# Seven-product form for half of the gate and value row blocks in a fused attention and SwiGLU kernel

## The chip, the cores and the metric

The kernel runs on one core of one Trainium2 chip. The metric is the time of one execution in device microseconds (us), median over several executions. In what follows PE is TensorE (matmuls), PEld its weight loads, DVE is VectorE, ACT is ScalarE and POOL is GpSimd. The tiles that matmuls write lie in PSUM (eight at a time in this kernel, called banks here), all other tiles of the engines in SBUF.

## The reference

A linear attention over 8 batches of 576 tokens is followed by a SwiGLU block over the 4608 tokens. The model width is 512, the hidden width 1536.

```python
# attention, per batch and head (8 x 8, 576 tokens, head size 64)
q_s = exp(q - max(q, -1)); q_s /= sum(q_s, -1)        # over the features
k_s = exp(k - max(k, 2));  k_s /= sum(k_s, 2)         # over the tokens
kv  = einsum('bhsd,bhse->bhde', k_s, v)
x   = einsum('bhsd,bhde->bhse', q_s, kv)              # -> (4608, 512)
# SwiGLU
g   = x @ w_gate                                      # (4608, 1536)
val = x @ w_val
out = (g * sigmoid(g) * val) @ w_out                  # (4608, 512)
```

## The kernel before

The kernel keeps x transposed (`xt`, features on partitions) and computes the hidden layer by 12 row blocks ("units") of 128 hidden features. One unit of 512 tokens is eight matmuls of 512 columns, a Silu on ScalarE and a multiply on VectorE:

```python
def m_unit(c0, n, m):                      # cut: splitting of n > 512
    for w, nm in ((wg, "g_ps"), (wv, "u_ps")):
        for kk in range(KT):               # KT = 4
            nc.tensor.matmul(out=p_, lhsT=w[:, kk, ms], rhs=xt[:, kk, c:c + w_], ...)
    nc.scalar.activation(out=sg, in_=g_ps, func=AF.Silu)
    nc.vector.tensor_mul(hr[:, m, r:r + w_], sg, u_ps)
```

The out-projection of 512 tokens (`o_quad`) is already done in a seven-product form: a product of two 2 x 2 block matrices takes seven block products in place of eight, if sums of blocks of both operands are made beforehand. The sums of the weight blocks (`wt`) are made once, on GpSimd; the sums of the hidden layer (`hs`) once per chunk, on VectorE. Several products add up in one PSUM bank, and some of these partial sums are wanted for themselves, so they are copied out between two products:

```python
def w_sums(eng):                           # called with GpSimd, in the stage of 448 tokens
    eng.tensor_sub(wt[:, 0], b12, b11);      eng.tensor_sub(wt[:, 1], b22, wt[:, 0])
    eng.tensor_sub(wt[:, 2], b22, b12);      eng.tensor_sub(wt[:, 3], b21, wt[:, 1])

def h_sum(Q, i, ...):                      # i = 0..3, one 128x1536 VectorE operation each

# o_quad: order of the products (each on two banks, p = 0, 1)
prod(x_, raw_h(0,0), raw_w(0,0));  ACT copies s1
prod(w,  sum_h(0),   sum_w(0));    ACT copies s5
between(0)                         # exps and casts of a later batch
prod(x_, sum_h(1),   sum_w(1));    DVE copies s2
prod(y,  raw_h(1,0), raw_w(1,0));  DVE adds
prod(x_, sum_h(2),   sum_w(2));    DVE adds s5
between(1)
prod(w,  sum_h(3),   raw_w(1,1));  DVE adds s2
prod(x_, raw_h(1,1), sum_w(3));    DVE copies
```

The frame: a prologue with the attention of batch 0, all units of batch 0 (576 tokens), a stage of 448 tokens that fills up to token 1024, and then seven chunks of 512 tokens. In each chunk the out-projection of the chunk before comes after unit 3, behind the four h sums that follow units 0 to 3. In the 448-token stage and the first five chunks ("attention chunks") the kv and x of a later batch are also computed, after units 8 and 10:

```python
chunks = [(S, 448)] + [(c, 512) for c in range(1024, n_tok, 512)]
for ci, (c0, n) in enumerate(chunks):
    # cut: steps = {8: kv_pair(b), 10: x_pair(b)} for b < B
    for m in range(MT):                    # MT = 12
        if ci > 0 and m == 4:
            o_quad(ci, between)
        m_unit(c0, n, m)
        if ci == 0 and m == 5:
            w_sums(nc.gpsimd)
        if ci > 0 and m < 4:
            h_sum(ci, m)
        if m in steps:
            steps[m]()
```

The softmax here doesn't subtract the row's maximum and nothing guards it: scores larger than these inputs give would overflow.

## Time and profile before

| | us |
|---|---|
| median of the runs | 309.9 |
| span of the profiled execution | 308.0 |
| PE busy | 302.4 |
| 448-token stage | 20.63 |
| an attention chunk | 31.87 |
| a chunk without attention | 29.89 |

Stage lengths are differences of start times in the timeline: the first matmul of the 448-token stage starts at 53.55 us, and the first one of each out-projection at 81.09, 112.96, 144.83, 176.70, 208.57 and 240.44, so the five chunks after the first out-projection have one length to the hundredth.

These lines of the page give the span and the busy time, and, last, the shares of the chain of waits (the chain of work that ended last):

```profile
span 308.0 us, 5679 instructions
...
PE 302.4 (98%) x2200; PEld 183.1 (59%) x2200; DVE 204.1 (66%) x395; ACT 144.1 (47%) x232; POOL 55.7 (18%) x42
...
PE 93%; DVE 4%; DMA 1%; ACT 0%; issue 0%
```

PE is busy 98% of the span. The list of PE's waits (waiting line, what released it, total us, times, longest) has two entries:

```profile
PE warm_ps L255 <- DVE zero L464: 1.1, 1, 1.1
PE kv L190 <- DVE vb L112: 0.2, 1, 0.2
```

So no steady-state wait exists.

The chunk is 31.87 us of 31.87 us PE. In the 448-token stage GpSimd makes the four `wt` sums, 3.09 us each.

### The profile page before, as it was taken

What the parts mean: (1) busy time and instruction counts of PE and PEld (TensorE: products, weight loads), DVE (VectorE), ACT (ScalarE), POOL (GpSimd) and SP (SyncE); (2) the same over time, 40 slices, a digit from 0 to 9 for tenths busy, and PEclk for the clock granted to TensorE, in tenths of its full rate; (3) what the DMA queues carried; (4) which work ended last, traced back from release to release, by engine and by line L of the source; (5) the groups of instructions that cost most, each with busy time, mean ns of one, the idle gap of its engine ahead of it and who ended that gap; (6) DMA issues with size and microseconds to landing.
All of it is one profiled execution on the core that took longest, in us unless ns stands there. A gap on an engine that the chain in (4) does not pass through costs nothing.

```text
span 308.0 us, 5679 instructions
## 1 busy us (share of the span) xinstructions
PE 302.4 (98%) x2200; PEld 183.1 (59%) x2200; DVE 204.1 (66%) x395; ACT 144.1 (47%) x232; POOL 55.7 (18%) x42
## 2 busy tenths in 40 slices
PE   8999999999999999999999999999999999999994
PEld 6777855454675458455844485448544764485443
DVE  3944459967867886788687768776877653664422
ACT  4753387824493439333944385347634213322300
POOL 1840014189420121102020302020200000000000
PEclk9999999999999999999999999999999999999999
DMA  7999999749019910894089506960540050006014
GB/s 262 263 185 207 250 393 391 221 89 393 24 31 203 385 59 0 177 321 180 0 165 294 217 2 144 285 247 2 119 97 0 0 121 19 0 2 136 3 34 103
DMA packets 39180, 46.39 MB, mean 151 GB/s; under 512 B 16368, under 2 KB 22384, under 8 KB 39152
## 3 DMA queue, kind: packets, MB, share of 16 engines
q1 hardware_dynamic: 33104, 41.17, 45.6%
q0 software_dynamic: 5808, 4.72, 9.8%
q8 instruction: 17, 0.28, 0.4%
q10 hardware_dynamic: 240, 0.13, 0.2%
q14 instruction: 11, 0.09, 0.1%
HBM read 37.75 MB, written 9.44 MB: 153 GB/s over the span
## 4 chain that ended last, share of the span: by engine, by line
PE 93%; DVE 4%; DMA 1%; ACT 0%; issue 0%
PE g_ps L304 31%; PE u_ps L304 30%; PE ox L383 12%; PE ow L383 6%; PE o_ps L331 5%; PE oy L383 3%; PE kv L190 3%; DMA q<-in_q_dram 1%; DVE rs L137 1%; PE o_ps L445 1%; PE xa L272 1%; DVE qs L146 1%; DVE xt L232 0%; DVE qt L112 0%; PE xz L272 0%; ACT eq L121 0%
## 5 line engine op out<-in xcount | busy, mean ns | idle before, releaser
L312 ACT ACTIVATE sg<-g_ps 128x512 f32<-128x512 f32 (+2 forms) x120 | 65.1, 554 | 124.3 <-PE g_ps L304 116.9
L313 DVE TENSOR_TENSOR hr<-sg,u_ps 128x512 bf16<-128x512 f32 (+2 forms) x120 | 74.2, 631 | 60.9 <-PE u_ps L304 60.4
L304 PE MATMUL g_ps<-xt,wg 128*128 128x512 bf16 (+2 forms) x480 | 111.6, 358 | 0.2
L304 PE MATMUL u_ps<-xt,wv 128*128 128x512 bf16 (+2 forms) x480 | 111.0, 358 | 0.0
L304 PEld LDWEIGHTS <-wv 128*128 128x128 f16 x480 | 46.9, 98 | 46.9 <-issue 0.3
L304 PEld LDWEIGHTS <-wg 128*128 128x128 f16 x480 | 45.9, 98 | 44.8 <-issue 2.2
L112 POOL CAST vb<-v 128x1152 bf16<-128x1152 f32 x14 | 19.6, 1398 | 103.5 <-DMA v<-in_v_dram 42.2
L383 PEld LDWEIGHTS <-hs 128*128 128x128 bf16 x336 | 32.9, 98 | 3.8
L383 PEld LDWEIGHTS <-hr 128*128 128x128 bf16 x252 | 24.7, 98 | 4.3
L137 DVE TENSOR_REDUCE rs<-eq 128x18 f32<-128x1152 bf16 x16 | 21.5, 1346 | 6.3 <-ACT eq L121 6.3
L146 POOL TENSOR_TENSOR qs<-eq,rr 128x1152 bf16<-128x1152 bf16 x7 | 14.8, 2121 | 58.2 <-DVE rr L141 49.1
L383 PE MATMUL ox<-wt,hs 128*128 128x256 f16 x168 | 20.6, 273 | 0.0
L121 ACT ACTIVATE eq<-q 128x1152 bf16<-128x1152 f32 x16 | 18.0, 1158 | 2.7 <-DMA q<-in_q_dram 2.6
L121 ACT ACTIVATE ek<-k 128x1152 bf16<-128x1152 f32 x16 | 18.0, 1152 | 2.0 <-DMA k<-in_k_dram 2.0
L331 PE MATMUL o_ps<-wo,hr 128*128 128x512 f16 x84 | 18.8, 379 | 0.0
L214 DVE TENSOR_SCALAR kn<-kv,kvr 64x64 bf16<-64x64 f32 x56 | 15.9, 283 | 1.3
L417 DVE COPY s<-ox 128x256 f32<-128x256 f32 x14 | 5.9, 425 | 12.8 <-PE ox L383 12.8
L146 DVE TENSOR_TENSOR qs<-eq,rr 128x1152 bf16<-128x1152 bf16 x9 | 13.5, 1498 | 0.4 <-DVE rr L141 0.2
L331 PEld LDWEIGHTS <-hr 128*128 128x128 bf16 x84 | 8.1, 98 | 9.5 <-issue 0.2
L255 PE MATMUL warm_ps<-zero 128*128 128x256 bf16 x80 | 11.2, 307 | 1.1 <-DVE zero L464 1.1
L190 PEld LDWEIGHTS <-ek 64*128 64x128 bf16 x288 | 8.4, 94 | 3.6 <-issue 2.5
L255 PEld LDWEIGHTS <-zero 128*128 128x128 bf16 x80 | 8.6, 110 | 3.1 <-DVE zero L464 1.1
(61 smaller groups left out, 230.8 us busy)
## 6 DMA issues: line engine op xcount, KB each, us to landing
q<-in_q_dram SPq DMA_DIRECT2D x16, 576.0 KB, 7.1
k<-in_k_dram SPq DMA_DIRECT2D x16, 576.0 KB, 8.5
v<-in_v_dram SPq DMA_DIRECT2D x16, 576.0 KB, 9.5
out_dram<-o_sb SPq DMA_DIRECT2D x70, 128.0 KB, 2.4
wo<-in_moe_w_out_dram POOLq DMA_DIRECT2D x3, 512.0 KB, 18.0
wg<-in_moe_w_gate_dram POOLq DMA_DIRECT2D x2, 512.0 KB, 11.1
wv<-in_moe_w_val_dram POOLq DMA_DIRECT2D x2, 512.0 KB, 12.8
wg<-in_moe_w_gate_dram POOLq DMA_DIRECT2D x2, 256.0 KB, 5.3
```

The source lines that it names most:

```text
L112: eng.tensor_copy(out=out, in_=in_)
L121: nc.scalar.activation(out=s["e" + what], in_=raw[what, b, G].rearrange("p h (t d) -> p t h d", d=64), func=AF.Exp,)
L137: nc.vector.reduce_sum(out=rs, in_=s["eq"].rearrange("p t h d -> p (t h) d"), axis=mybir.AxisListType.X)
L146: eng.tensor_mul(s["qs"].rearrange("p t (h d) -> p (t h) d", d=64), s["eq"].rearrange("p t h d -> p (t h) d"), s["rr"].to_broadcast([128, ...
L190: nc.tensor.matmul(out=s["kv"][g][:, 0:129], lhsT=s["ek"][r, t, :, :].rearrange("p h d -> p (h d)"), rhs=s["vb"][r, t, 0:129], start=(t == 0),
L214: nc.vector.tensor_scalar_mul(out_, src, sc)
L255: nc.tensor.matmul(out=ps[:, 0:256], lhsT=zero[:, 0:128], rhs=zero, start=True, stop=True)
L304: nc.tensor.matmul(out=p_[:, 0:w_], lhsT=w[:, kk, ms], rhs=xt[:, kk, c:c + w_], start=(kk == 0), stop=(kk == KT - 1),)
L312: nc.scalar.activation(out=sg[:, 0:w_], in_=g_ps[:, 0:w_], func=AF.Silu)
L313: nc.vector.tensor_mul(hr[:, m, r:r + w_], sg[:, 0:w_], u_ps[:, 0:w_])
L331: nc.tensor.matmul(out=o_ps, lhsT=hr[:, m, r0:r0 + 128], rhs=wo[:, m, :], start=(m == 0), stop=(m == MT - 1),)
L383: nc.tensor.matmul(out=dst[p][:, 0:HN], lhsT=lhs(kk, p), rhs=rhs(kk), start=start and kk == 0, stop=kk == HM - 1, skip_group_check=True,)
```

## The change

The intent is to take PE columns away. Six of the 12 units of each 512-token chunk are now computed as three "cycles", each of which makes the gate and the value of two row blocks by the seven-product form: 28 matmuls of 256 columns in place of 16 of 512. The form needs sums of gate and value weights (`gt`, once, VectorE, in the 448-token stage), sums of x (`xs`, once per chunk, GpSimd), and copies and adds of partial sums. Since the last product of a cycle accumulates into a bank from which a partial sum must first be read, it is put off (`pend`) to the middle of the next cycle, and the third one to `flush()` before the units that stay direct. A direct unit (`md`) runs inside each cycle to give the copies time. The out-projection moves to the start of each chunk, its product into y moves forward, and h sums 0, 1 and 3 move into it. The diff, cut to its core:

```diff
+    def g_sums(eng):                      # four lambdas, wg and wv blocks
+        ... eng.tensor_sub(gt[:, 0], b12, b11) ... gt[:, 3]
+    def x_sum(c0, i, eng=nc.vector): ...  # xs[0..3], 128x512 each
+    def cycle(c0, n, md, mid=None, slot=None):
+        prod(bx, wg[:, 0:2], xa(0, 0), True)
+        nc.scalar.copy(out=s1, in_=bx)
+        prod(by, wg[:, 2:4], xa(0, 1), True)
+        prod(bw, gt[:, 0], xs[0], True)
+        nc.scalar.copy(out=s5, in_=bw)
+        flush()                            # last product of the cycle before
+        nc.vector.tensor_add(s1, by, s1)
+        nc.scalar.activation(out=sa, in_=s1, func=AF.Silu)
+        ... mid(), slot()
+        direct(wg, g_ps)                   # unit md
+        prod(bx, gt[:, 1], xs[1])
+        nc.scalar.copy(out=s2, in_=bx)
+        nc.scalar.activation(out=sd, in_=g_ps, func=AF.Silu)
+        prod(bw, wv[:, 2:4], xs[3])
+        nc.vector.tensor_add(s2, bw, s2)
+        nc.gpsimd.tensor_mul(h_out(0), halves(sa), halves(s2))
+        direct(wv, u_ps)
+        prod(bx, gt[:, 2], xs[2])
+        nc.vector.tensor_add(s5, bx, s5)
+        nc.vector.tensor_mul(hr[:, md, rh:rh + 512], sd, u_ps)
+        def last():
+            prod(bx, gt[:, 3], xa(1, 1))
+            nc.scalar.activation(out=sb, in_=bx, func=AF.Silu)
+            nc.gpsimd.tensor_mul(h_out(1), halves(sb), halves(s5))
+        pend.append(last)
     # o_quad
+        between(0)                         # h sums 0 and 1, q exps, casts
+        prod(y, raw_h(1, 0), raw_w(1, 0))  # was after the s2 copy
         prod(w, sum_h(0), sum_w(0)); copies s5
-        between(0)
+        between(1)                         # k exps
         prod(x_, sum_h(1), sum_w(1)); copies s2
-        prod(y, raw_h(1, 0), raw_w(1, 0))
+        between(2)                         # h sum 3
         prod(x_, sum_h(2), sum_w(2))
     # stage of 448 tokens
+        w_adds = g_sums(nc.vector)
+            if m == 9: x_pair(2)           # was after unit 10
+            if m == 10: h_sum(1, 2); four x sums on GpSimd
+            if 4 <= m < 8: w_adds[m - 4]()
     # chunks
+            o_quad(ci, between)
+            cycle(c0, 0, 6, slot=norm_1 if att else None)
+            cycle(c0, 1, 7)
+            cycle(c0, 2, 8, mid=(lambda: kv_pair(b)) if att else None)
+            flush()
+            m_unit(c0, 512, 9)
+            if att: x_pair(b)
+            m_unit(c0, 512, 10)
+            ... four x sums on GpSimd, h_sum(ci + 1, 2)
+            m_unit(c0, 512, 11)
# cut: xt as a ring of 1536 tokens in fp16, kn in one operation per group
# in place of two, more buffers for sg and s, norm_mul of group 1 on GpSimd
```

More of the change, by code (lines that the diff above doesn't have):

```diff
@@ L49 @@
     HN = d_model // 2
+    XR = 1536
+    NS = 3
+    SD = 2 * NS * 128
     WARM = (64, 8, 8)
@@ L54 @@
     at = ctx.enter_context(tc.tile_pool(name="at", bufs=2))
-    ff = ctx.enter_context(tc.tile_pool(name="ff", bufs=3))
+    ff = ctx.enter_context(tc.tile_pool(name="ff", bufs=4))
     ob = ctx.enter_context(tc.tile_pool(name="ob", bufs=5))
-    sn = ctx.enter_context(tc.tile_pool(name="sn", bufs=1))
+    sn = ctx.enter_context(tc.tile_pool(name="sn", bufs=2))
     psp = ctx.enter_context(tc.tile_pool(name="psp", bufs=8, space=bass.MemoryType.PSUM))
@@ L67 @@
     hs = const.tile([128, 4, HM, 256], BF16, name="hs", tag="hs")
-    xt = const.tile([128, KT, n_tok], BF16, name="xt", tag="xt")
+    xt = const.tile([128, KT, XR], FP16, name="xt", tag="xt")
+    gt = const.tile([128, 4, 2, SD], FP16, name="gt", tag="gt")
+    xs = [const.tile([128, 2, 256], FP16, name=f"xs{i}", tag=f"xs{i}") for i in range(4)]
     hr = const.tile([128, MT, RING], BF16, name="hr", tag="hr")
@@ L76, in load @@
     def load(b, G, what, src, after=None):
-        raw[what, b, G] = ld.tile([128, 2, T * 64], FP32, tag=what, name=what)
+        raw[what, b, G] = ld.tile(
+            [128, 2, T * 64], FP32, tag=what, name=what, bufs=2 if what == "v" else 3
+        )
         ap = bass.AP(
@@ L206, in kn, with ring_parts, put_x @@
         if "kn" not in s:
-            s["kn"] = at.tile([128, 2, 64], BF16, tag="kn", name="kn")
-        for h in range(2):
-            r = slice(64 * h, 64 * h + 64)
-            out_, src, sc = s["kn"][r, g, :], s["kv"][g][r, r], s["kvr"][r, g:g + 1]
-            if eng is nc.scalar:
-                nc.scalar.mul(out_, src, sc)
-            else:
-                nc.vector.tensor_scalar_mul(out_, src, sc)
+            s["kn"] = at.tile([128, 2, 128], BF16, tag="kn", name="kn")
+        out_, src, sc = s["kn"][:, g, :], s["kv"][g][:, 0:128], s["kvr"][:, g:g + 1]
+        if eng is nc.scalar:
+            nc.scalar.mul(out_, src, sc)
+        else:
+            nc.vector.tensor_scalar_mul(out_, src, sc)
+    def ring_parts(c0, n, ring):
+        c1 = c0 + n
+        while c0 < c1:
+            w_ = min(c1, (c0 // ring + 1) * ring) - c0
+            yield c0 % ring, w_
+            c0 += w_
+    def put_x(eng, k0, c0, src):
+        o = 0
+        for r, w_ in ring_parts(c0, src.shape[-1], XR):
+            copy(eng, xt[:, k0, r:r + w_], src[:, o:o + w_])
+            o += w_
     def x(b, G, piece, eng=nc.scalar):
@@ L225, in x @@
                     out=xp[h][64 * g:64 * g + 64, 0:n].rearrange("p (t c) -> p t c", c=64),
-                    lhsT=s["kn"][r, g, :],
+                    lhsT=s["kn"][r, g, r],
                     rhs=s["qt"][g][r, t0:t1, :],
@@ L230, in x @@
         c0 = b * S + 64 * t0
-        copy(eng, xt[:, 2 * G, c0:c0 + n], xp[0][:, 0:n])
-        nc.vector.tensor_copy(out=xt[:, 2 * G + 1, c0:c0 + n], in_=xp[1][:, 0:n])
+        put_x(eng, 2 * G, c0, xp[0][:, 0:n])
+        put_x(nc.vector, 2 * G + 1, c0, xp[1][:, 0:n])
     def x_both(b, G, eng=nc.scalar):
@@ L273, in x_pair @@
                             out=o[64 * g:64 * g + 64, :].rearrange("p (t c) -> p t c", c=64),
-                            lhsT=s["kn"][r, g, :],
+                            lhsT=s["kn"][r, g, r],
                             rhs=s["qt"][g][r, t0:t1, :],
@@ L278, in x_pair @@
             for h, eng in ((0, nc.scalar), (1, nc.vector)):
-                copy(eng, xt[:, 2 * G + h, c0:c0 + n_a], ps[G][h][:, 0:n_a])
+                put_x(eng, 2 * G + h, c0, ps[G][h][:, 0:n_a])
         for h, eng in ((0, nc.scalar), (1, nc.vector)):
-            copy(
-                eng,
-                xt[:, h:h + 2 * NG - 1:2, c0 + n_a:c0 + S],
-                z[h].rearrange("p (g c) -> p g c", g=NG),
-            )
+            o = 0
+            for r, w_ in ring_parts(c0 + n_a, n_z, XR):
+                copy(
+                    eng,
+                    xt[:, h:h + 2 * NG - 1:2, r:r + w_],
+                    z[h].rearrange("p (g c) -> p g c", g=NG)[:, :, o:o + w_],
+                )
+                o += w_
     def kv_pair(b):
@@ L304, in m_unit @@
                     nc.tensor.matmul(
-                        out=p_[:, 0:w_], lhsT=w[:, kk, ms], rhs=xt[:, kk, c:c + w_],
+                        out=p_[:, 0:w_], lhsT=w[:, kk, ms], rhs=xt[:, kk, c % XR:c % XR + w_],
                         start=(kk == 0), stop=(kk == KT - 1),
@@ L313, in m_unit, with flush @@
             nc.vector.tensor_mul(hr[:, m, r:r + w_], sg[:, 0:w_], u_ps[:, 0:w_])
+    pend = []
+    def flush():
+        while pend:
+            pend.pop()()
+    def g_sums(eng):
+        b11, b12 = wg[:, 0:2, 0:SD], wv[:, 0:2, 0:SD]
+        b21, b22 = wg[:, 2:4, 0:SD], wv[:, 2:4, 0:SD]
+        return [
+            lambda: eng.tensor_sub(gt[:, 0], b12, b11),
+            lambda: eng.tensor_sub(gt[:, 1], b22, gt[:, 0]),
+            lambda: eng.tensor_sub(gt[:, 2], b22, b12),
+            lambda: eng.tensor_sub(gt[:, 3], b21, gt[:, 1]),
+        ]
@@ new lines, in x_sum, with halves, prod, direct @@
+    def x_sum(c0, i, eng=nc.vector):
+        r = c0 % XR
+        a11, a12 = xt[:, 0:2, r:r + 256], xt[:, 2:4, r:r + 256]
+        a21, a22 = xt[:, 0:2, r + 256:r + 512], xt[:, 2:4, r + 256:r + 512]
+        if i == 0:
+            eng.tensor_add(xs[0], a21, a22)
+        elif i == 1:
+            eng.tensor_sub(xs[1], xs[0], a11)
+        elif i == 2:
+            eng.tensor_sub(xs[2], a11, a21)
+        else:
+            eng.tensor_sub(xs[3], a12, xs[1])
+    def cycle(c0, n, md, mid=None, slot=None):
+        r, rh = c0 % XR, c0 % RING
+        m0 = 2 * n
+        def halves(t):
+            return t.rearrange("p (j c) -> p j c", j=2)
+        def prod(bank, wgt, rhs, first=False):
+            for j in range(2):
+                c = slice(128 * (m0 + j), 128 * (m0 + j) + 128)
+                for kk in range(2):
+                    nc.tensor.matmul(
+                        out=bank[:, 256 * j:256 * j + 256], lhsT=wgt[:, kk, c], rhs=rhs[:, kk, :],
+                        start=first and j == 0 and kk == 0, stop=kk == 1, skip_group_check=True,
+                    )
+        def direct(w, ps):
+            for kk in range(KT):
+                nc.tensor.matmul(
+                    out=ps, lhsT=w[:, kk, 128 * md:128 * md + 128], rhs=xt[:, kk, r:r + 512],
+                    start=(kk == 0), stop=(kk == KT - 1),
+                )
+        def xa(t, c):
+            return xt[:, 2 * c:2 * c + 2, r + 256 * t:r + 256 * t + 256]
+        def h_out(t):
+            return hr[:, m0:m0 + 2, rh + 256 * t:rh + 256 * t + 256]
+        def sg_tile():
+            return ff.tile([128, 512], FP32, tag="sg", name="sg")
+        bx, by, bw = [f_tile(n_) for n_ in ("sx", "sy", "sw")]
+        s1, s2, s5 = [sn.tile([128, 512], FP32, tag=n_, name=n_) for n_ in ("s1", "s2", "s5")]
+        prod(bx, wg[:, 0:2], xa(0, 0), True)
[5 more added lines that the diff above has]
+        nc.vector.tensor_add(s1, by, s1)
+        sa = sg_tile()
+        nc.scalar.activation(out=sa, in_=s1, func=AF.Silu)
+        if mid is not None:
+            mid()
+        if slot is not None:
+            slot()
+        g_ps, u_ps = f_tile("g_ps"), f_tile("u_ps")
+        direct(wg, g_ps)
+        prod(bx, gt[:, 1], xs[1])
+        nc.scalar.copy(out=s2, in_=bx)
+        sd = sg_tile()
+        nc.scalar.activation(out=sd, in_=g_ps, func=AF.Silu)
[8 more added lines that the diff above has]
+            prod(bx, gt[:, 3], xa(1, 1))
+            sb = sg_tile()
+            nc.scalar.activation(out=sb, in_=bx, func=AF.Silu)
+            nc.gpsimd.tensor_mul(h_out(1), halves(sb), halves(s5))
+        pend.append(last)
@@ L372, in o_quad @@
         s1, s2, s5 = [
-            [sn.tile([128, HN], FP32, tag=f"{n}{p}", name=n) for p in range(2)]
-            for n in ("s1", "s2", "s5")
+            [t[:, HN * p:HN * p + HN] for p in range(2)]
+            for t in [sn.tile([128, 512], FP32, tag=n, name=n) for n in ("s1", "s2", "s5")]
         ]
@@ L408, in o_quad @@
             nc.scalar.copy(out=s1[p], in_=x_[p][:, 0:HN])
-        for p in range(2):
-            prod(w, p, sum_h(0), sum_w(0), True)
-        for p in range(2):
-            nc.scalar.copy(out=s5[p], in_=w[p][:, 0:HN])
         between(0)
-        for p in range(2):
-            prod(x_, p, sum_h(1), sum_w(1), False)
-        for p in range(2):
-            nc.vector.tensor_copy(out=s2[p], in_=x_[p][:, 0:HN])
         for p in range(2):
@@ L422, in o_quad @@
         for p in range(2):
+            prod(w, p, sum_h(0), sum_w(0), True)
+        for p in range(2):
+            nc.scalar.copy(out=s5[p], in_=w[p][:, 0:HN])
+        between(1)
+        for p in range(2):
+            prod(x_, p, sum_h(1), sum_w(1), False)
+        for p in range(2):
+            nc.vector.tensor_copy(out=s2[p], in_=x_[p][:, 0:HN])
+        between(2)
+        for p in range(2):
             prod(x_, p, sum_h(2), sum_w(2), False)
@@ L425, in o_quad @@
             add(p, 1, 1, x_, s5)
-        between(1)
+        between(3)
         for p in range(2):
@@ L549 @@
         exp(2, 1, "k")
-        chunks = [(S, 448)] + [(c, 512) for c in range(1024, n_tok, 512)]
-        for ci, (c0, n) in enumerate(chunks):
-            b = ci + 2
-            steps = {}
-            if b < B:
-                steps = {8: lambda: kv_pair(b), 10: lambda: x_pair(b)}
-            def between(i):
-                if b >= B:
+        w_adds = g_sums(nc.vector)
+        for m in range(MT):
+            if m == 4:
+                norm_sum(2, 1)
+                norm_mul(2, 1, nc.gpsimd)
+                tr_dma(2, 1)
+                load_group(3, 0)
+                load_group(3, 1)
+            m_unit(S, 1024 - S, m)
+            if m == 5:
+                w_sums(nc.gpsimd)
+            if m == 8:
+                kv_pair(2)
+            if m == 9:
+                x_pair(2)
+            if m == 10:
+                h_sum(1, 2)
+                for i in range(4):
+                    x_sum(1024, i, nc.gpsimd)
+            if 4 <= m < 8:
+                w_adds[m - 4]()
+        n_ch = n_tok // 512 - 1
+        for ci in range(1, n_ch):
+            b, c0 = ci + 2, 512 * (ci + 1)
+            att = b < B
+            def between(i):
+                if i == 0:
+                    h_sum(ci, 0)
+                    h_sum(ci, 1)
+                elif i == 2:
+                    h_sum(ci, 3)
+                if not att:
                     return
@@ L562, in between, with norm_1 @@
                         exp(b, G, "q")
+                        cast_v(b, G, nc.gpsimd)
+                elif i == 1:
                     for G in range(NG):
                         exp(b, G, "k")
-                        cast_v(b, G, nc.gpsimd)
-                else:
+                elif i == 3:
                     norm_sum(b, 0)
                     norm_mul(b, 0, nc.gpsimd)
-            for m in range(MT):
-                if ci == 0 and m == 4:
-                    norm_sum(2, 1)
-                    norm_mul(2, 1, nc.gpsimd)
-                    tr_dma(2, 1)
-                    load_group(3, 0)
-                    load_group(3, 1)
-                if ci > 0 and m == 4:
-                    o_quad(ci, between)
-                    if b < B:
-                        tr_dma(b, 0)
-                if ci > 0 and m == 5 and b < B:
-                    norm(b, 1)
-                    tr_dma(b, 1)
-                    if b + 1 < B:
-                        load_group(b + 1, 0)
-                        load_group(b + 1, 1)
-                m_unit(c0, n, m)
-                if ci == 0 and m == 5:
-                    w_sums(nc.gpsimd)
-                if ci > 0 and m < 4:
-                    h_sum(ci, m)
-                if m in steps:
-                    steps[m]()
+                    tr_dma(b, 0)
+            def norm_1():
+                norm_sum(b, 1)
+                norm_mul(b, 1, nc.gpsimd)
+                tr_dma(b, 1)
+                if b + 1 < B:
+                    load_group(b + 1, 0)
+                    load_group(b + 1, 1)
+            o_quad(ci, between)
[4 more added lines that the diff above has]
+            m_unit(c0, 512, 9)
+            if att:
+                x_pair(b)
+            m_unit(c0, 512, 10)
+            if ci + 1 < n_ch:
+                for i in range(4):
+                    x_sum(c0 + 512, i, nc.gpsimd)
+                h_sum(ci + 1, 2)
+            m_unit(c0, 512, 11)
         last = n_tok // 128 - 4
```

## The prediction

> **What bounds the kernel now.** TensorE. The page gives PE 302.4 us busy of a 308.0 us span at granted clock 1.0. PE's own waits sum to about 1.3 us, and the chain of waits is 93% PE. In the timeline a 512-column matmul follows the next every 0.216 us (0.863 per four), a 256-column one every 0.109 (1.31 per twelve): only fewer columns or new stalls move the time. A chunk with attention takes 31.87 us, one without 29.9. VectorE (66%), ScalarE (47%) and GpSimd (18%) are hidden behind eight PSUM banks.
>
> **Removed.** Each of 21 cycles (7 chunks x 3) replaces 16 matmuls of 512 columns (3.45 us) by 28 of 256 (3.06 us): 0.395 us each, 8.3 us in all, all of it on the critical path.
>
> **Added, hidden.** Per cycle three ScalarE copies (0.58 each, as the 128x512 o_ps copy), three VectorE adds for two multiplies (0.69 each), two GpSimd multiplies of about 1.0 us (estimate from 3.09 us for 1536 columns); per chunk about 4.1 us of x sums on GpSimd. No engine is full.
>
> **Added, not hidden.** The seven products share three banks, so PE now waits for evacuations in the middle of a sum. From the instruction order and measured durations (PE to VectorE or ScalarE takes 0.26 us):
> - Flush after the third cycle: the last product accumulates into the bank that VectorE must first read for s5, directly after the product before it. Nothing stands between: 0.26 + 0.69 + semaphore, about 1.0 us x 7 = 7 us.
> - First cycle of the five attention chunks: ScalarE loads the Silu table (1.28 us) and runs one Silu before copying s2, which PE needs 0.8 us earlier: about 4 us.
> - Out-projection: oy no longer stands between the s2 copy and the next product into the same bank, and the fourth h sum (0.95 us) starts only after both s2 copies. About 0.1 + 0.4 us x 7 = 3.2 us.
> - h sums 0 and 1 now follow the last unit's multiply, beside the x sums on GpSimd. The Trainium skill, "SBUF — State Buffer", section "SBUF: two separate sides", says that VectorE operations with two SBUF inputs and GpSimd operations lock each other out; the trace agrees in kind (h sums 0.95 us alone, 1.29 to 1.34 beside a GpSimd cast). Perhaps 1 us in all.
>
> The sum is -8.3 + 7 + 4 + 3.2 + 1 = about +6.5 us.
>
> **Predicted: 316.5 us**, 8 in 10 between 312.0 and 320.5. Chances: faster by over 2% 0.06, within 2% 0.45, slower by over 2% 0.49.
>
> **What would show it.** Pitch of matmuls unchanged, fewer columns. In the waits list, PE (or its weight load) waits for the VectorE s5 add, 7 times about 1.0 us; for the ScalarE s2 copy, 5 times about 0.8; and for the s2 copy and the fourth h sum in the out-projection, 7 times 0.4 to 0.6. The chain of waits holds several per cent of VectorE and ScalarE. An attention chunk takes about 33 us, one without about 30.3. If these waits are missing, the time falls towards 302.
>
> **What would make it wrong.** The s5 stall dominates: if the bank dependency is shorter than I think, the result is near 309. If GpSimd multiplies of fp32 run much slower than 1.0 us, or lock VectorE out for longer, the rotation of the s and sg buffers delays ScalarE and the loss grows beyond 320. At chunk 0 the four new VectorE weight sums may stall x of batch 2 for some tenths.

The terms of its sum add up to +6.9 us; the text rounds them to "about +6.5".

## More of the kernel before

The next view gives the busy time of each engine in two stretches (start:end, length, then PE, PEld, DVE, ACT and POOL busy with instruction counts, granted PE clock, DMA share, GB/s): first the 448-token stage, then the span from one out-projection to the next.

```profile
53.55:74.18 20.63, 20.54 (x148) 10.63 (x148) 17.22 (x35) 11.53 (x20) 12.39 (x5) 1.00 0.70 216
112.96:144.83 31.87, 31.87 (x234) 18.84 (x232) 23.87 (x47) 16.79 (x25) 4.41 (x3) 1.00 0.57 164
```

## The result and the profile after

The changed kernel takes 327.8 us (median of four runs, 327.34 to 328.55) against 309.9 for the kernel before. The ratio is 1.0576, with a 95% interval of 1.0551 to 1.0602. Ratios here are the mean time of one kernel's fast runs over that of the other's in the same rounds, so they are not quite the ratio of the medians quoted. The result is slower by over 2%, which the prediction gave a chance of 0.49, but it lies 7 us above the upper end of its range.

From the page: span, busy times, PE's busy tenths and the granted clock in 40 slices of 8.1 us, and the chain's shares.

```profile
span 325.5 us, 6279 instructions
...
PE 302.3 (93%) x2452; PEld 206.6 (63%) x2452; DVE 222.6 (68%) x390; ACT 173.9 (53%) x294; POOL 165.0 (51%) x117
...
PE   8999999956999899989998999899989998999895
...
PEclk9999999985999999999999999999999999999999
...
PE 77%; DVE 14%; ACT 5%; issue 3%; DVEq 0%; ACTq 0%
```

PE's busy time has not fallen, in spite of the removed columns (the half clock below adds 2.9 us of it, and a group of matmuls ahead of a wait is counted longer, as told further down), and PE now stands idle for 23 us. Both the hole in PE and the hole in the granted clock are in the ninth and tenth slice, that is at 65 to 81 us: in the 448-token stage, which the arithmetic of the change does not touch at all. The same stretches as before:

```profile
53.14:83.40 30.26, 23.46 (x152) 11.15 (x149) 28.40 (x37) 11.81 (x21) 21.48 (x9) 0.83 0.58 186
116.77:150.17 33.40, 31.54 (x269) 22.11 (x268) 24.73 (x45) 21.14 (x34) 20.69 (x15) 1.00 0.59 156
```

The ledger by stages, from the start times of each stage in the two timelines:

| stage | before | after | difference |
|---|---|---|---|
| prologue and batch 0 | 53.55 | 53.14 | -0.41 |
| 448 tokens | 20.63 | 30.26 | +9.63 |
| five attention chunks, each | 31.87 | 33.46 (mean) | +1.59, five times +7.93 |
| sixth chunk | 29.89 | 30.68 | +0.79 |
| seventh chunk | 29.89 | 29.96 | +0.07 |
| tail | 14.69 | 14.18 | -0.51 |
| span | 308.0 | 325.5 | +17.5 |

PE's waits in the changed kernel (the same columns as before; the wait of the first matmul and a short one are left out):

```profile
PE sx L376 <- DVE s L423: 6.3, 7, 1.2
PE xa L290 <- DVE kn L219: 2.8, 1, 2.8
PE sx L376 <- ACT s L415: 2.7, 5, 0.5
PE u_ps L325 <- DVE hr L334: 2.2, 1, 2.2
PE ox L501 <- DVE hs L481: 2.0, 6, 0.3
PE kv L197 <- DVE hr L334: 1.5, 1, 1.5
```

and of the weight load:

```profile
PEld L501 <- DVE hs L481: 3.7, 6, 0.6
...
PEld L501 <- DVE hs L485: 2.4, 7, 0.4
```

L423 is the s5 add at the end of a cycle, L415 the s2 copy behind the table load, L481 and L485 are h sums 1 and 3. These come back from chunk to chunk, and all four were in the prediction. The three waits that occur once (2.8, 2.2 and 1.5 us) lie in the 448-token stage. This is what the timeline shows there (start, length, engine, line, operation, tiles, count, and in brackets the idle time before and its releaser):

```profile
64.31 3.80 POOL L466 TENSOR_TENSOR wt<-wo 128x1536 f16<-128x1536 f16 x1
...
65.61 3.31 DVE L347 TENSOR_TENSOR gt<-wv,gt 128x1536 f16<-128x1536 f16 x1
...
68.18 3.68 POOL L467 TENSOR_TENSOR wt<-wo,wt 128x1536 f16<-128x1536 f16 x1
...
69.37 3.31 DVE L348 TENSOR_TENSOR gt<-wv 128x1536 f16<-128x1536 f16 x1
...
69.50 0.68 PE L197 MATMUL kv<-vb,ek 64*128 64x129 bf16 x17 [1.52 <-DVE hr L334]
...
73.27 1.65 PE L325 MATMUL u_ps<-xt,wv 128*128 128x448 f16 x4 [2.22 <-DVE hr L334]
...
77.75 0.48 PE L290 MATMUL xa<-qtd,kn 64*64 64x320 bf16 x4 [2.83 <-DVE kn L219]
```

A `gt` sum on VectorE takes 3.31 us here (the first of the four, beside another multiply on GpSimd, 2.69). The same operation takes 0.94 us where the GpSimd sums are cut into short pieces (experiment a2 below). Each one ends 0.81 or 0.82 us after the GpSimd operation beside it has ended: the second `wt` sum ends at 68.18 + 3.68 = 71.86, the third `gt` sum at 69.37 + 3.31 = 72.68. A VectorE operation of 0.94 us that waited until the GpSimd operation was over would look nearly so. The `wt` sums take 3.7 to 3.8 us here, where they took 3.09 before, so GpSimd waits as well. This is the lock of the Trainium skill, "SBUF — State Buffer", section "SBUF: two separate sides": a VectorE operation with two SBUF inputs and a GpSimd operation that reads SBUF exclude each other for the whole instruction. Four of these sums leave VectorE about 9 us behind (12.6 us in place of 3.8), and the evacuations of PSUM wait behind them in VectorE's queue. PE stands until one of them is done: the three waits above are for VectorE's multiply (L334) and for `kn` (L219).

The clock adds to it. Busy time and granted clock (the column before the last two) in three single microseconds of the same kernel:

```profile
70.00:71.00 1.00, 1.00 (x11) 0.41 (x6) 1.00 (x1) 0.00 (x0) 1.00 (x1) 1.00 1.00 380
71.00:72.00 1.00, 0.05 (x1) 0.00 (x0) 1.00 (x1) 0.54 (x1) 1.00 (x2) 0.73 1.03 406
72.00:73.00 1.00, 0.00 (x0) 0.00 (x0) 1.00 (x2) 0.00 (x0) 1.00 (x1) 0.50 1.05 406
```

The granted clock falls to half at about 71.5 us and is back at 1.0 at about 81.7 us; in between four matmuls of 448 columns take 1.65 us, where they take 0.92 elsewhere. The added 9.63 us are 6.7 us of PE idle time (6.80 against 0.09) and 2.9 us of longer PE work (23.46 against 20.54).

One attention chunk now takes 33.40 us. Without any wait it would take 31.87 - 3 x 0.395 = 30.69 us (an estimate from the matmul durations of the trace before, as in the prediction). The 2.7 us between are three waits (1.02, 0.71 and about 1.0 us), counted from where PE could have issued the next matmul. (PE's busy time of 31.54 us makes them look shorter: four matmuls before a wait are counted as 0.60 us, to the end of the last one, while they are issued over 0.437.) The first is at the flush:

```profile
142.38 0.60 PE L376 MATMUL sx<-xs,gt 128*128 128x256 f16 x4
...
143.09 0.69 DVE L423 TENSOR_TENSOR s<-sx,s 128x512 f32<-128x512 f32 x1 [0.44 <-PE sx L376]
...
143.84 0.60 PE L376 MATMUL sx<-xt,gt 128*128 128x256 f16 x4 [0.85 <-DVE s L423]
```

Four matmuls of 256 columns are issued over 0.437 us, so PE could have gone on at 142.82 and went on at 143.84: 1.02 us. This is the price of reading a partial sum where nothing stands between the two products: 0.27 us until VectorE starts, 0.69 us of the add, and the semaphore. The second wait is in the first cycle, where ScalarE loads the Silu table:

```profile
129.11 1.28 ACT L407 ACT_TABLE_LOAD   x1
...
130.40 0.63 ACT L407 ACTIVATE sg<-s 128x512 f32<-128x512 f32 x1
...
130.94 0.57 ACT L415 COPY s<-sx 128x512 f32<-128x512 f32 x1
...
131.56 0.60 PE L376 MATMUL sx<-xs,gt 128*128 128x256 f16 x4 [0.55 <-ACT s L415]
```

PE's direct matmuls before it end their issue at 130.85, so this costs 0.71 us. The third is the out-projection: it took 9.17 us of PE time from its first matmul to the first one behind it before, and takes 10.17 after. Its beginning:

```profile
115.73 1.15 POOL L359 TENSOR_TENSOR xs<-xs,xt 128x512 f16<-128x512 f16 x1
...
115.92 1.78 DVE L483 TENSOR_TENSOR hs<-hr 128x1536 bf16<-128x1536 bf16 x1
...
119.56 1.79 DVE L481 TENSOR_TENSOR hs<-hs,hr 128x1536 bf16<-128x1536 bf16 x1
...
121.41 2.82 PE L501 MATMUL ox<-wt,hs 128*128 128x256 f16 x24 [0.34 <-DVE hs L481]
```

The h sums, which take 0.95 us alone, take 1.78 and 1.79 us: again two-input VectorE operations beside two-input operations on GpSimd, this time the x sums.

### The profile page after: what moved, and what is told of

The parts are those of the page before. It is cut to its first block, busy times and chain, and to the rows that moved or that the text cites. A ratio compares the mean times of both kernels' runs of the same rounds, so it can differ in the third digit from the quotient of the medians.

```text
span 325.5 us, 6279 instructions
## 1 busy us (share of the span) xinstructions
PE 302.3 (93%) x2452; PEld 206.6 (63%) x2452; DVE 222.6 (68%) x390; ACT 173.9 (53%) x294; POOL 165.0 (51%) x117
## 4 chain that ended last, share of the span: by engine, by line
PE 77%; DVE 14%; ACT 5%; issue 3%; DVEq 0%; ACTq 0%
PE g_ps L325 11%; PE sx L376 11%; PE u_ps L325 11%; PE ox L501 9%; PE o_ps L449 6%; PE sw L376 5%; PE g_ps L383 4%; PE u_ps L383 4%; PE warm_ps L273 4%; PE ow L501 4%; DVE hs L481 3%; PE sy L376 3%; PE kv L197 3%; DVE hs L479 2%; DVE hr L334 2%
## 5 line engine op out<-in xcount | busy, mean ns | idle before, releaser
L334 DVE TENSOR_TENSOR hr<-sg,u_ps 128x512 bf16<-128x512 f32 (+3 forms) x57 | 31.2, 570 | 33.8 <-PE u_ps L325 31.7
L325 PE MATMUL u_ps<-xt,wv 128*128 128x320 f16 (+2 forms) x228 | 47.6, 341 | 2.2 <-DVE hr L334 2.2
L376 PEld LDWEIGHTS <-gt 128*128 128x128 f16 x336 | 32.8, 98 | 23.7 <-issue 11.6
L325 PE MATMUL g_ps<-xt,wg 128*128 128x320 f16 (+2 forms) x228 | 47.4, 338 | 0.2 <-ACT xt L117 0.2
L333 ACT ACTIVATE sg<-g_ps 128x512 f32<-128x512 f32 (+3 forms) x57 | 27.4, 506 | 36.6 <-PE g_ps L325 35.2
L420 POOL TENSOR_TENSOR hr<-sg,s 128x512 bf16<-128x512 f32 x21 | 26.7, 1271 | 37.2 <-DVE s L419 37.2
L429 POOL TENSOR_TENSOR hr<-sg,s 128x512 bf16<-128x512 f32 x21 | 26.6, 1269 | 26.6 <-ACT sg L428 26.6
L501 PEld LDWEIGHTS <-hs 128*128 128x128 bf16 x336 | 31.1, 97 | 11.8 <-DVE hs L481 3.7
L325 PEld LDWEIGHTS <-wv 128*128 128x128 f16 x228 | 22.6, 99 | 19.8 <-issue 3.8
L325 PEld LDWEIGHTS <-wg 128*128 128x128 f16 x228 | 21.7, 98 | 16.4 <-issue 3.3
L376 PE MATMUL sx<-xs,gt 128*128 128x256 f16 x168 | 25.2, 272 | 2.7 <-ACT s L415 2.7
L383 PE MATMUL g_ps<-xt,wg 128*128 128x512 f16 x84 | 21.6, 380 | 0.0
L383 PE MATMUL u_ps<-xt,wv 128*128 128x512 f16 x84 | 21.6, 379 | 0.0
L428 ACT ACTIVATE sg<-sx 128x512 f32<-128x512 f32 x21 | 12.6, 600 | 15.4 <-PE sx L376 15.4
```

What stands on the lines that cost most here:

```text
L325: nc.tensor.matmul(out=p_[:, 0:w_], lhsT=w[:, kk, ms], rhs=xt[:, kk, c % XR:c % XR + w_], start=(kk == 0), stop=(kk == KT - 1),)
L333: nc.scalar.activation(out=sg[:, 0:w_], in_=g_ps[:, 0:w_], func=AF.Silu)
L334: nc.vector.tensor_mul(hr[:, m, r:r + w_], sg[:, 0:w_], u_ps[:, 0:w_])
L376: nc.tensor.matmul(out=bank[:, 256 * j:256 * j + 256], lhsT=wgt[:, kk, c], rhs=rhs[:, kk, :], start=first and j == 0 and kk == 0, stop=kk ...
L383: nc.tensor.matmul(out=ps, lhsT=w[:, kk, 128 * md:128 * md + 128], rhs=xt[:, kk, r:r + 512], start=(kk == 0), stop=(kk == KT - 1),)
L420: nc.gpsimd.tensor_mul(h_out(0), halves(sa), halves(s2))
```

## The experiments

The theory: the two sets of weight sums lock each other out in the 448-token stage and this costs the 9.6 us; the chunks lose by the three kinds of wait above. Three other readings of the same traces compete with it, and the runs below tell them apart. R1, for the stage: x of batch 2 now follows one unit earlier, after unit 9 in place of 10, and its kv chain is simply not ready in time. R2, for the stage: the drop of the clock is a cause of its own, and would come without the lock. R3, for the chunks: GpSimd's multiplies, at 1.27 us above the estimate of 1.0, hold back the sg and s buffers, so that taking single waits away gains little. Each run was made beside runs of the kernel before on the same chip, which took 309.9 to 310.0 us; all results but that of b2 were correct. Gains are given against the 327.8 us of the changed kernel, which was not run again in these rounds; the kernel before, which was, agrees within 0.2 us.

### a1: the gate and value weight sums earlier, on GpSimd

```diff
+        w_adds = g_sums(nc.gpsimd)
         for m in range(MT):
             m_unit(0, S, m)
+            if m == 5:
+                for w_add in w_adds: w_add()
...
-        w_adds = g_sums(nc.vector)         # 448-token stage
-            if 4 <= m < 8:
-                w_adds[m - 4]()
```

> Changed kernel, but the four weight sums of the gate/value products run on GpSimd during batch 0, where GpSimd is idle, instead of on VectorE beside GpSimd's other weight sums. Theory (the two engines lock each other out in that stage, the backlog stalls PE and its clock drops): the stage of 448 tokens falls from 30.3 us to 20.6, granted clock back to 1.0, time 327.8 to about 318. Rival (the stage is long because x of batch 2 comes one unit earlier than before): the stage stays above 26 us and the time above 323.

Measured: 320.0 us, ratio 1.0317 (1.0293 to 1.0340). The 448-token stage fell from 30.26 to 20.52 us, with `x_pair(2)` still after unit 9, so R1 falls. But the time is 2 us above the 318 that were expected, and the first chunk grew from 33.37 to 36.84 us, beside 32.64 to 33.41 for the other four. The timeline shows why:

```profile
74.31 3.81 POOL L469 TENSOR_TENSOR wt<-wo,wt 128x1536 f16<-128x1536 f16 x1
...
75.74 3.20 DVE L479 TENSOR_TENSOR hs<-hr 128x1536 bf16<-128x1536 bf16 x1
...
78.99 2.48 PE L501 MATMUL ow<-wt,hs 128*128 128x256 f16 x12 [2.29 <-DVE hs L479]
```

With the stage shorter, the last `wt` sum on GpSimd ran into the first out-projection and locked an h sum, for which PE waited 2.3 us, and the mean granted clock of that chunk fell to 0.95. The lock had moved, not gone: the wait was relieved in one place and met in the next.

### a2: the out-projection weight sums in six pieces each

```diff
-        eng.tensor_sub(wt[:, 0], b12, b11)
+        for kk in range(HM):
+            eng.tensor_sub(wt[:, 0, kk], b12[:, kk], b11[:, kk])
... the same for wt 1 to 3
```

> Changed kernel, but each of GpSimd's four out-projection weight sums (1536 columns, 3.1 us alone) is cut into six of 256; VectorE still does the same four sums of 1536 in the same places. Theory (VectorE waits for the end of a whole GpSimd operation): its sums shorten from 3.3 us to 1.3 to 1.8, the PE stall of that stage mostly goes, time 319 to 321. Rival (VectorE simply has too many columns there, or the memory is shared evenly): sums stay above 2.7 us, time above 325.

Measured: 320.85 us, ratio 1.0350 (1.0327 to 1.0373), as expected. The columns on both engines are the same and only the length of one GpSimd instruction differs. VectorE now gets its turn between two pieces (timeline, six pieces grouped in the first line):

```profile
64.83 6.83 POOL L467 TENSOR_TENSOR wt<-wo 128x256 f16<-128x256 f16 x6
...
66.14 0.94 DVE L347 TENSOR_TENSOR gt<-wv,gt 128x1536 f16<-128x1536 f16 x1
```

The last three `gt` sums took 0.94 us each in place of 3.3, the stage 21.6 us in place of 30.26, and the granted clock was 1.0 throughout. DMA traffic is no rival either: in the same run the DMA share is 1.13 from 66 to 68 us and 0.82 from 68 to 70 (1 is full), while these sums run in 0.94 us. And R2 falls as well: where the lock's long waits are gone, the clock does not drop. The waits come first and the clock follows. The pieces have a price that the expectation did not name: the six pieces of the first `wt` sum took 0.66 to 1.43 us each beside VectorE's operations, most of the later ones 0.67, so GpSimd finished late and the first chunk grew from 33.37 to 35.03 us. PE's waits show it, all of them in that chunk:

```profile
PE ox L505 <- POOL wt L473: 1.1, 3, 0.4
PE sw L376 <- POOL xs L363: 1.0, 1, 1.0
```

### a3: the third cycle's last product after unit 9

```diff
-            flush()
             m_unit(c0, 512, 9)
+            flush()
```

> Changed kernel, but the last product of the third cycle is flushed after the direct unit 9 instead of before it. Theory (PE waits for the s5 add because nothing stands between two products into one bank): the seven waits of PE for it, 6.3 us with 0.85 each, go and the time falls by about 6 us to 322. Rival (the wait returns at the x banks or the h sums): less than 3 us gained.

Measured: 317.3 us, ratio 1.0229 (1.0211 to 1.0247): 10.5 us saved, where about 6 were expected. The waits for the s5 add are gone from the list, which is the expected part. The rest came from the out-projection, which fell from about 10.2 to 9.42 us in the second to the sixth chunk (in the first to 9.99; in the last it grew from 9.42 to 9.87). The timeline shows h sum 2 and GpSimd's second x sum just before the out-projection's first matmul:

```profile
148.71 0.95 DVE L483 TENSOR_TENSOR hs<-hr 128x1536 bf16<-128x1536 bf16 x1
148.74 1.93 POOL L359 TENSOR_TENSOR xs<-xs,xt 128x512 f16<-128x512 f16 x1
...
149.52 1.47 PE L501 MATMUL ox<-wo,hr 128*128 128x256 f16 x12
```

In the changed kernel this x sum started 0.19 us ahead of the h sum and the h sum took 1.78 us. Here the x sum comes 0.26 us later against the out-projection (0.78 us before it and not 1.04), presumably since GpSimd now has the multiply of the last product in its queue just before. The h sum therefore starts 0.03 us ahead, takes 0.95 us, and the x sum takes 1.93. The Trainium skill, "SBUF — State Buffer", section "Who interferes with whom", puts it as "Issue order, not op shape, decides who blocks", and this pair of lines agrees. Nothing in the edit concerned the h sums; this part of the gain, about 3.5 us, is luck: it hangs on which of two operations starts first by less than 0.2 us.

### a4: the Silu table loaded early

```diff
                     for G in range(NG):
                         exp(b, G, "k")
+                    nc.scalar.activation(out=warm, in_=warm, func=AF.Silu)
```

> Changed kernel, but a one-column Silu after the k exponentials brings the table load ahead of the first cycle. Theory (the load sits between two copies that PE waits for): the five waits for the s2 copy, 0.55 us each, go and the time falls by about 2.7 us to 325. Rival (the load then delays the s1 copies as much): no gain.

Measured: 324.7 us, ratio 1.0477 (1.0452 to 1.0502), close to the 325 expected. A Silu of one column right after the last exp pulls the load out of the cycle, and the waits for the s2 copy are gone:

```profile
125.61 1.28 ACT L713 ACT_TABLE_LOAD   x1
...
126.91 0.20 ACT L713 ACTIVATE warm<-warm 128x1 f32<-128x1 f32 x1
```

### b1: both sets of weight sums early

This is a1 with the `wt` sums moved as well, into gaps of GpSimd's work between batch 0 and the 448-token stage.

```diff
+        o_adds = w_sums(nc.gpsimd)         # now four lambdas
+        o_adds[0](); o_adds[1]()
         cast_v(1, 0, nc.gpsimd); cast_v(1, 1, nc.gpsimd)
+        o_adds[2]()
...
         cast_v(2, 0, nc.gpsimd)
+        o_adds[3]()
         cast_v(2, 1, nc.gpsimd)
...
-            if m == 5:
-                w_sums(nc.gpsimd)          # 448-token stage
```

> Changed kernel, but both groups of weight sums (gate/value and out-projection) run on GpSimd before the stage of 448 tokens. Theory (lock between the two engines): the 2.3 us wait of PE for the first h sum, and the low clock, that moving the gate/value sums alone left in the first out-projection, go too; first two stages 20.6 + 33.4 us, time 320.0 to about 316.6, clock 1.0. Rival (the first chunk is slow for another reason): no better than 319.

Measured: 316.0 us, ratio 1.0206 (1.0188 to 1.0224). The stage takes 20.52 us and the first chunk 32.69. Of the 11.8 us gained in time, the profile puts 9.7 in the stage: that is what the place of the weight sums cost. Another 1.8 us come from the chunks, mostly because the first two out-projections fell from about 10.2 to 9.52 and 9.42 us. There h sum 2 now starts ahead of the second x sum (at 105.70 us against 105.88 in the second chunk) and takes 0.95 us: the same luck of order as in a3, and no part of the theory.

### b2: no x sums in the chunks (wrong result)

The x sums of the first chunk are used for all. The result is wrong (relative error 1.55); PE's work is the same.

```diff
             if ci + 1 < n_ch:
-                for i in range(4):
-                    x_sum(c0 + 512, i, nc.gpsimd)
                 h_sum(ci + 1, 2)
```

> Wrong result on purpose: changed kernel in which the x sums are formed once and not again in each chunk, so that GpSimd does not run them beside the h sums. Theory (the x sums on GpSimd lock VectorE's h sums out at the chunk's start): the out-projection falls from 10.17 us to 9.4 to 9.5 in six chunks, time 327.8 to about 323.5. Rival (its whole loss is the new order of the products): it stays at 10.1 and the time moves less than 1 us.

Measured: 324.6 us, ratio 1.0469 (1.0443 to 1.0495), 3.2 us less than the changed kernel; 4.3 were expected. PE's waits for h sums 0 and 1 nearly vanish. Of the six out-projections that took 10.1 to 10.2 us, four now take 9.41 or 9.42 (the first two 9.49 and 9.78), and what remains in them is the late fourth h sum (2.3 us of weight-load waits in all). So the lock between x sums and h sums costs 3 to 4 us (3.2 in time, 4.0 in the out-projections of the two profiles), 0.75 per out-projection where it strikes.

### b3: b1, a3 and a4 together

> The three mends together: both weight sums early, flush after unit 9, Silu table early. If the losses add, 316.6 - 10.5 - 3.1 = 303 us, 2% below the kernel before. If they share a cause, 306 or more.

Measured: 303.0 us, ratio to the kernel before 0.9778 (0.9763 to 0.9792). The single gains against the changed kernel, 11.8 (b1), 10.5 (a3) and 3.1 (a4), sum to 25.4; together they gave 24.8. The causes are thus nearly independent, though not to the tenth: the shorter first two out-projections (0.9 us of the profile of a3, 1.4 of that of b1) are in both gains. R3 falls: with these three waits gone no hidden limit by GpSimd shows, though its multiplies still take 1.27 us each. POOL is the fullest it gets, 179.2 of 301.0 us by the page. The one wait left that comes back in every chunk, from the list of the weight load's waits:

```profile
PEld L503 <- DVE hs L487: 2.4, 7, 0.4
```

### b4: the out-projection after the first cycle

The last known wait is the fourth h sum in the out-projection (L487 above). Here the out-projection follows the first cycle, its products stand in the order of the kernel before, h sums 0 and 1 are made during that cycle, and x sum 3 before x sum 2.

```diff
# on top of b3
+            def h01(): h_sum(ci, 0); h_sum(ci, 1)
+            cycle(c0, 0, 6, slot=h01)
             o_quad(ci, between)            # between(0): flush(), h sums 2 and 3
-            cycle(c0, 0, 6, slot=norm_1 if att else None)
-            cycle(c0, 1, 7)
+            cycle(c0, 1, 7, slot=norm_1 if att else None)
...
-                for i in range(4):
+                for i in (0, 1, 3, 2):
                     x_sum(c0 + 512, i, nc.gpsimd)
-                h_sum(ci + 1, 2)
```

> As the three mends together, and the out-projection after the first cycle, in the order of products of the kernel before, with its first two h sums during that cycle. Theory (out-projection first leaves VectorE no time for the h sums): the out-projection takes 9.17 us plus 0.44 for the flushed product, no wait for h sums, time about 301.5. Rival (the x sums are then late for the first cycle): PE waits for GpSimd, time 303 or more.

Measured: 302.4 us, ratio 0.9761 (0.9746 to 0.9775), the fastest version of all, if 0.9 us above the 301.5 that were expected. The busy line of its page:

```profile
PE 293.9 (98%) x2452; PEld 207.3 (69%) x2452; DVE 209.4 (70%) x386; ACT 174.6 (58%) x299; POOL 167.3 (56%) x121
```

and the busy times of one of its attention chunks, from one out-projection to the next:

```profile
109.17:139.96 30.79, 30.79 (x271) 22.40 (x268) 24.67 (x45) 21.25 (x35) 19.23 (x14) 1.00 0.58 167
```

The waits for h sums are gone, and this chunk takes 30.79 us, all of it PE, against the 30.69 of the estimate without waits (the five take 30.68 to 30.99, those of b3 30.93 to 31.02). Beside b3 the gain in time is not sure, as the two intervals overlap; it is the waits list that shows the difference.

## Why the prediction was wrong

The direction was the more likely of those it gave (0.49, against 0.45 for no change beyond 2%), and nearly all parts of its mechanism stand. The size was wrong mainly because of one step (9.6 of the 10.6 us that were missed).

- **The failed step** is the last sentence, "At chunk 0 the four new VectorE weight sums may stall x of batch 2 for some tenths." Measured are 9.63 us in the profile, and with the sums elsewhere the stage falls back to 20.52 us (a1, b1). The prediction did cite the lock, but applied it to the h sums alone and not to the pair that collides longest: four VectorE sums of 128x1536 put next to four GpSimd sums of 128x1536 that already stood in the same stage of the kernel before. The sum held no term for it. Worked out, each VectorE sum beside a GpSimd sum of 3.1 us should have been given some 3 us, not 0.94, in a stage in which VectorE was already busy 17.2 of 20.6 us. That the result would be a half clock on top (2.9 of the 9.6 us) would not have followed from the trace before.
- **Removed PE work: right.** 0.395 us per cycle. b4 shows it: chunks of 30.68 to 30.99 us, where the estimate is 30.69; the changed kernel hid it under waits.
- **The s5 wait at the flush: right**, 1.0 predicted, 1.02 measured in the timeline in six of seven chunks, and 0.35 more in one (6.3 in the list, where the longest is 1.2). a3 removes it.
- **The s2 copy behind the table load: right**, 0.8 predicted, 0.71 measured in the timeline, five times; a4 gains 3.1 us.
- **The out-projection: right in kind, under-sized.** Predicted 0.46 us for the copy and the fourth h sum, and 0.14 for the locks ("Perhaps 1 us in all"), per chunk; measured 1.0 in an attention chunk. b2 divides it: the x sums on GpSimd cost 0.75, the rest 0.25. These locks cost 3 to 4 us in all and not 1.
- **GpSimd's multiplies: under-sized without effect**, 1.27 us measured against an estimate of 1.0. Its fear that this holds VectorE or the buffers back did not come true in the chunks, as b3 shows.
- **The ledger closes.** Predicted +6.9, profile +17.5. The difference of 10.6 is 9.6 (the stage of 448 tokens), 1.9 (five attention chunks at +1.59 in place of +1.21) and -0.9 (a shorter prologue and tail, of which the prediction said nothing).

What stays open: a1 spared only 7.8 us of time where the profile shows 9.7 gone from the stage, because its first chunk is 3.5 us longer (and later ones 1.1 shorter), but I did not separate the part of that chunk that the low clock takes from the part of the lock. The stage also varies where its code is unchanged: 30.26 us in the changed kernel, 31.02 in a3, 31.32 in a4 and 29.98 in b2. So gains of single runs are not sure to some tenths; in a4 the five attention chunks are 3.5 us shorter together, while the time fell by 3.1. And no run tells exactly what rule the clock follows.

## What to carry to other kernels

When a change adds operations with two SBUF inputs to VectorE or GpSimd, look in the timeline for what stands on the other of the two engines at that place, and count each VectorE operation as long as the GpSimd operation beside it; a small operation made once can cost more than the whole steady-state saving. Put such one-time sums where PE does not wait for VectorE, as b1 does, or cut the GpSimd ones into short pieces; in a2 this freed VectorE, but GpSimd then finished late. A product that continues a bank whose partial sum must first be read needs other matmuls between, here one unit of 512 tokens, and then the seven-product form gives nearly what its column count promises: 302.4 us against 309.9, 7.5 of the 8.3 us.

## What the Trainium skill lacked or had wrong

- "SBUF — State Buffer", sections "SBUF: two separate sides" and "Who interferes with whom": right, and its rule of issue order was seen from both sides (h sum 1.78 us when 0.19 us late, 0.95 when 0.03 us early, with the x sum at 1.93). Lacking is the remedy that a2 shows: the lock is held per instruction, so cutting the GpSimd sum of 128x1536 into six of 128x256 brought VectorE's sum from 3.31 to 0.94 us, while single pieces beside VectorE's operations took up to 1.43 us, where most of the later ones took 0.67.
- "TensorE: Matmul & The Clock Gate", section "Part 1: The HAM clock gate (the "warmup" mystery)": it says that the clock halves after an idle window of about 3.4 us. Here it halved at about 71.5 us, when the longest single wait had been 1.5 us, then 1.6 us of work, then some 0.4 us of idleness; and no single wait of that stage was longer than 2.8 us. So less than one full idle window was enough in this run, and the clock was back at 1.0 only some 10 us later. A later section of that page tells of a kernel whose many short idle times made the clock swing, but gives no lengths for them.
- "ScalarE: Activation LUTs", section "What ACT_TABLE_LOAD costs": it adds a drain of about 1.38 us to the load of 1.28 us. The load took 1.28 us here as well, but the next operation started 1.29 us (129.11 to 130.40) and 1.30 us (125.61 to 126.91) after the load's start, so no drain showed after it; and in a4 the load began 0.02 us after the end of the exp before it, so none showed before it either.
- "PSUM — Partial Sum Buffer", section "PSUM: the matmul accumulator": it allows a read in the middle of an accumulation group but gives no cost. Here it cost PE 1.02 us for 512 fp32 columns read by VectorE, when the next product into the bank followed directly.
- "GPSIMD Engine Reference", section "3.1 Elementwise — side-by-side cycle accounting": it has a measured time for a two-input add of fp32 on GpSimd at one size, but none for a multiply or for 512 columns; a multiply of 128x512 fp32 inputs into bf16 took 1.27 us here.
